# Four attention layers on one core: wol moved into the wo block's slot, wq cut in rows of 2, 2, 1, and the values of the last heads moved forward

## The chip, the core and the metric

The kernel runs on one core of a Trainium2 chip. The metric is device time in microseconds (us) of that core. TensorE is called PE, VectorE DVE, ScalarE ACT; SP is the engine whose queue issues the transfers. PE's granted clock is the share of its full speed that it gets at a moment; in these traces it is 1.0 or 0.5.

## The reference

One token passes four layers: A, B, A, B. Each layer is a norm, a query projection, attention over a cache of 8192 positions in 32 heads of 192, and an output projection.

```python
def attn(x, k_cache, v_cache, wq, wo):           # A and B have the same shapes
    q = (x @ wq).reshape(1, 1, 32, 192).transpose(0, 2, 1, 3)
    p = softmax(einsum("bhqd,bhkd->bhqk", q, k_cache) * 192 ** -0.5)
    o = einsum("bhqk,bhkd->bhqd", p, v_cache)
    return o.transpose(0, 2, 1, 3).reshape(1, 1, 32 * 192) @ wo

x = A_x                                           # 1 x 1 x 640, bfloat16
x = x + attn(layernorm(x), A_k, A_v, A_wq, A_wo)  # "layer 0"
x = x + attn(layernorm(x), B_k, B_v, B_wq, B_wo)  # "layer 1"
x = x + attn(layernorm(x), A_k, A_v, A_wq, A_wo)  # "layer 2"
x = x + attn(layernorm(x), B_k, B_v, B_wq, B_wo)  # "layer 3"
```

One K or V of a head is 3.15 MB. Six such tiles of layers 0 and 1 are kept on the chip for layers 2 and 3; all else is read again.

## The kernel before

SBUF holds a pool of eight slots of one K or V each. A plan lists all transfers in order, and SP issues each as soon as the earlier holders of its slot are done with it. The steps list what the engines do. Here are the parts that the change touches (cuts are marked).

```python
KEPT = {0: {("k", 0), ("v", 0)}, 1: {("v", 28), ("v", 29), ("v", 30), ("v", 31)}}
...
    Q_PARTS = [[(0, 2), (2, 2), (4, 1)] if l < 2 else [(0, 1), (1, 2), (3, 2)] for l in range(NL)]
    NB = 3
...
            elif l == 2:
                plan += [("wq", l, g) for g in range(3)]     # three parts of wq, then K of head 1
                steps.append(("wq", l, 0))
...
                if l == 2 and p == 0:
                    part = [("m", l, 0), ("wq", l, 1), ("s", l, 0), ("v", l, 0), ("wq", l, 2)]
                elif p < H - AHEAD:
                    part = [("m", l, p), ("s", l, p), ("v", l, p)]   # products with K, softmax, values
                else:
                    part = [("m", l, p)]
                    if p > H - AHEAD:
                        part.append(("s", l, p - 1))
                    if p == H - 1:
                        part.append(("s", l, p))
                        part += [("v", l, i) for i in range(H - AHEAD, H)]
                        part.insert(-O_LAST, ("wc", l, 2))
...
        for n in plan:
            if n[0] == "wol" and n[1] + 1 < NL:              # wol shares a slot with the next layer's wq
                m = ("wq", n[1] + 1, 0)
                allot(m)
                before[n] = before[("wq", n[1] + 1, 2)] if n[1] == 0 else before[m]
...
            def q_spread(h):
                c0 = h * DH
```

"wo" is a block of ten heads' rows of the output weights, "wol" the two last heads' rows, "wob" the part of layer 3's last block that is loaded by itself. In layers 2 and 3 wq comes in three parts; a row of it is one of the five rows that each partition holds, 1.47 MB. In layer 2 the slot for K of head 1 is the one that kept K of head 0 holds, so its transfer waits for the products ("m") of head 0 in layer 2.

Of the kernel before, what the change touches and what calls it, by code (L numbers as in the profile page):

```python
# [63 lines left out]
HEADS_W = 10  # L64
# [3 lines left out]
AHEAD = 4  # L68
# [3 lines left out]
def build(nc, A_x, A_k, A_v, A_wq, A_wo, B_x, B_k, B_v, B_wq, B_wo, out):  # L72
# [13 lines left out]
    QW = H * DH  # L86
    Q_PARTS = [[(0, 2), (2, 2), (4, 1)] if l < 2 else [(0, 1), (1, 2), (3, 2)] for l in range(NL)]
    O_PART = [P] * NL
    OI = [O_LAST * DH // n for n in O_PART]
    NB = 3  # L90
    G = 4
# [6 lines left out]
    with ExitStack() as ctx:  # L98
# [14 lines left out]
        oT = sb("oT", [P, NW], BF16)  # L113
        oTl = sb("oTl", [P, max(OI)], BF16)
        o_sb = sb("o_sb", [P, 2 * DH], F32)
# [81 lines left out]
        for l in range(NL):  # L197
            if l < 2:
                plan.append(("wq", l, 0))
                steps += [("wq", l, g) for g in range(3)]  # L200
            elif l == 2:
                plan += [("wq", l, g) for g in range(3)]
                steps.append(("wq", l, 0))
            else:
                plan.append(("wq", l, 0))
                steps.append(("wq", l, 0))
            for p in range(H):
                if p in (HEADS_W, 2 * HEADS_W):
                    b = p // HEADS_W - 1
                    steps += [("wc", l, b), ("wo", l, b)]  # L210
                    plan.append(("wo", l, b))
                if first_load("k", l, p) == ("k", l, p):
                    plan.append(("k", l, p))
                if stays("k", l, p):
                    plan.append(("t", l, p))
# [3 lines that stand above are left out]
                    part = [("m", l, p), ("s", l, p), ("v", l, p)]  # L219
                else:  # L220
                    part = [("m", l, p)]
                    if p > H - AHEAD:
                        part.append(("s", l, p - 1))
                    if p == H - 1:
                        part.append(("s", l, p))
                        part += [("v", l, i) for i in range(H - AHEAD, H)]
                        part.insert(-O_LAST, ("wc", l, 2))
                steps += part
                plan += [n for n in part if n[0] == "v" and first_load(*n) == n]
                if l == 3 and p == 1:  # L230
                    for g in (1, 2):
                        plan.append(("wq", l, g))
                        steps.append(("wq", l, g))
            plan.append(("wo", l, 2))
            steps.append(("wo", l, 2))
            plan.append(("wol", l))
            steps.append(("wol", l))
        plan.append(("wob", NL - 1))
        at = {n: i for i, n in enumerate(steps)}

        def released(n):

            if n[0] in "kvt":
                l, p = n[1:]
                if n[0] != "t" and stays(*n):
                    l, p = n[1] + 2, ORDER[n[1] + 2]["heads"].index(head(*n[1:]))
                return at[("v" if n[0] == "v" else "m", l, p)]
            return at[n]
# [15 lines left out]
        for n in plan:  # L264
            if n[0] == "wol" and n[1] + 1 < NL:
                m = ("wq", n[1] + 1, 0)
                allot(m)
                before[n] = before[("wq", n[1] + 1, 2)] if n[1] == 0 else before[m]
            elif n[0] == "wob":
                before[n] = []  # L270
            elif n not in place:
                allot(n)
# [4 lines left out]
        def wq_rows(l, g):  # L277

            c0, k = Q_PARTS[l][g]
            if l < 2:  # L280
                i = place[("wq", l, 0)] * TS
                return pool[:, i + c0 * QW:i + (c0 + k) * QW].rearrange("p (c n) -> p c n", c=k)
            return slot[place[("wq", l, g)]][:, 0:k * QC].rearrange("p (c n) -> p c n", c=k)

        def wol_rows(l):

            if l + 1 == NL:
                i = place[("wol", l)] * TS
            else:
                i = place[("wq", l + 1, 0)] * TS + (DC * QW if l == 0 else QC)  # L290
            return pool[0:O_PART[l], i:i + OI[l] * D]

        def transfer(n):
# [4 lines left out]
            if n[0] == "wol":  # L298
                r0 = o["wol"] * DH
                if O_PART[l] == P:  # L300
                    return SP.op(lambda s: s.dma_start(
                        wol_rows(l), w["wo"][r0:r0 + O_LAST * DH].rearrange("(p i) n -> p (i n)", p=P)),
                        *free, sem=semOL, inc=16)
                k = O_PART[l] // O_LAST
                for h in range(O_LAST):
                    e = SP.op(lambda s, h=h: s.dma_start(
                        wol_rows(l)[h * k:(h + 1) * k],
                        w["wo"][r0 + h * DH:r0 + (h + 1) * DH].rearrange("(q e i) n -> e q (i n)", e=8, i=OI[l])),
                        *free, sem=semOL, inc=16)
                return e  # L310
            if n[0] == "t":
# [13 lines left out]
            elif n[0] == "wq":  # L325
                c0, k = Q_PARTS[l][n[2]]
                f = lambda s: s.dma_start(
# [52 lines left out]
        def layer(l, ev_z, ev_true):  # L380
# [36 lines left out]
            def q_columns(g):  # L417

                n = ("wq", l, g)
                c0, k = Q_PARTS[l][g]  # L420
                t3 = wq_rows(l, g)[:, :, ORDER[l]["q1"] if l < 2 else 0:]
# [16 lines left out]
            def q_spread(h):  # L438

                c0 = h * DH  # L440
                PE.wait(last["qT"], last["QB"], ev_const)
# [15 lines left out]
            def project(n, rows, o, ev_o):  # L457

                t3 = rows.rearrange("p (i n) -> p i n", n=D)
                k = t3.shape[1]  # L460
                end = n == ("wob", l) or n == ("wol", l) and l + 1 < NL
                PE.wait(ev_o, need(n), last["YB"])
                for i in range(k):
                    for c in range(DC):
                        e = PE.op(lambda t, i=i, c=c, f=y_first[0], fin=end and i == k - 1: t.matmul(  # L465
                            YB[:, c:c + 1], lhsT=t3[:, i, c:D:DC], rhs=o[:, i:i + 1], start=f, stop=fin,
                            skip_group_check=True), signal=(i == k - 1 and c == DC - 1), bank=use["YB"])
                        y_first[0] = False
                freed[n] = e
                return e  # L470
# [65 lines left out]
            def values(h):  # L536
# [16 lines left out]
                if h < H - O_LAST:  # L553
                    parts = [(o_sb[:], OB[par][:, 0:2 * DH])]
                else:
                    q = 1 if O_PART[l] == P else O_PART[l] // O_LAST // 8
                    parts = [(o_sb[:, i * DH:(i + 1) * DH].rearrange("p (i e q) -> p q e i", i=OI[l], q=q),
                              OB[par][:, i * DH:(i + 1) * DH].rearrange("p (q e i) -> p q e i", i=OI[l], q=q))
                             for i in range(2)]
                for o, i in parts:  # L560
                    ev_os[h] = AC.op(lambda a, o=o, i=i: a.activation(o, i, ACT.Copy, scale=rl[pi][:, 0:1]),  # L561
                                     e, ev_rl[h], last["osb"], bank=use[f"O{par}"])
                last["O"][par] = last["rl"][pi] = ev_os[h]

            def gather(h):
# [6 lines left out]
                last["osb"] = e  # L572
                o0 = (h % HEADS_W) * DH
                last["TO"] = last["row_written"] = AC.op(
                    lambda a: a.activation(orow[0:1, o0:o0 + DH], TB[0:1, C_O:C_O + DH], ACT.Copy), e, last["orow"], bank=use["TB"])  # L575

            def gather_last(h):

                n = O_PART[l] // O_LAST
                k = OI[l]  # L580
                r0 = (h - (H - O_LAST)) * n
# [14 lines left out]
            for i, n in enumerate(here):  # L596
# [15 lines left out]
                elif n[0] == "wc":  # L612
                    todo()
                    todo = None
                    columns(NW)
                    last["oTw"] = last["TT"]
                elif n[0] == "wo":
# [3 lines left out]
                    k = NW - NB if n == ("wo", NL - 1, 2) else NW  # L621
                    last["oT"] = project(n, slot[place[n]][:, 0:k * D], oT[:, 0:k], last["oTw"])
                else:
                    last["TT"] = last["TTn"]
                    last["oTl"] = ev_y = project(n, wol_rows(l), oTl[0:O_PART[l]], last["TTn"])
                    if l + 1 == NL:
                        ev_y = project(("wob", l), slot[place[("wo", l, 2)]][:, (NW - NB) * D:NW * D], oT[:, NW - NB:NW], last["oTw"])
                following = [m[2] for m in here[i + 1:] if m[0] == "m" and m[2] not in ev_q][:1]
# [68 lines left out]
```

## Time and profile before

| | |
|---|---|
| time | 1997.24 us, median of 3 (1996.39 to 1998.24) |
| moved by the transfer queue q1 | 848.38 MB, busy 99.4% of the span |
| PE, DVE, ACT busy | 70%, 53%, 11% |

These lines are from the page of the kernel before: the span; the rate in 40 equal slices of 49.9 us; and the queue with packets, MB and its share of sixteen engines' time.

```profile
span 1994.7 us, 20412 instructions
...
GB/s 410 431 431 428 432 429 429 430 431 430 428 430 431 428 432 428 431 429 429 431 382 431 428 431 428 431 430 429 431 429 427 430 430 429 430 429 429 429 432 345
...
q1 hardware_dynamic: 40256, 848.38, 99.4%
```

The kernel is bound by its transfers. Nearly every slice moves 427 to 432 GB/s. Three do not: the first, the 21st and the last. The 21st holds the border of layers 1 and 2. These are its 5 us windows; the columns are the window, its length, then busy time and instructions of PE, PE's weight loads, DVE, ACT and POOL, then PE's granted clock, the transfers' share and GB/s.

```profile
1015.00:1020.00 5.00, 3.44 (x78) 2.96 (x70) 0.00 (x0) 1.11 (x3) 0.00 (x0) 1.00 0.54 227
1020.00:1025.00 5.00, 3.95 (x53) 2.95 (x52) 1.23 (x10) 0.00 (x0) 0.54 (x1) 0.55 0.63 224
1025.00:1030.00 5.00, 3.87 (x53) 1.23 (x44) 4.48 (x3) 0.73 (x2) 0.00 (x0) 0.50 1.00 418
1030.00:1035.00 5.00, 5.00 (x51) 0.89 (x33) 2.88 (x3) 0.00 (x0) 0.00 (x0) 0.92 1.00 422
1035.00:1040.00 5.00, 4.14 (x95) 2.88 (x96) 0.78 (x4) 0.44 (x2) 0.00 (x0) 0.76 1.05 438
```

For about 9 us the rate is halved. The two lines below are the transfer queue's timeline there (start, length, what is issued).

```profile
997.38 29.25 SPq L327 DMA_DIRECT2D pool<-in_A_wq_dram  x3
1034.40 0.34 SPq L322 DMA_DIRECT2D pool<-in_A_k_cache_dram  x1
```

The first line merges three issues: one row of wq at 997.38, and after a long wait two rows at 1021.05 and two at 1026.24. The wait is for the projection of the last wo block, whose slot the second part takes. PE's timeline shows what that projection and the steps after it do; the bracket names the idle time before a line and what ended it.

```profile
1017.86 3.16 PE L465 MATMUL YB<-oT,pool 128*128 128x1 bf16 x75 [0.51 <-DMA pool<-in_B_wo_dram]
...
1024.83 1.39 PE L427 MATMUL QT<-xb,pool 128*128 128x1 bf16 x45
...
1027.34 0.61 PE L508 MATMUL S<-pool,ident 128*128 128x512 bf16 x1 [1.13 <-DVE pool L495]
1027.74 6.63 PE L58 MATMUL S<-pool,ident 128*128 128x512 bf16 x23
```

The projection (first line) waited for the landing of wo, not for PE. The column sums of wq, which make q with 45 matmuls for each row (second line), and the products of head 0 (the last two) follow. When the products end at 1034.37, K of head 1 is issued.

One thing the views above do not print is in the trace's record of semaphore updates. Each transfer reports sixteen times, once for each engine. For the row of wq ahead of the wait the reports come at:

```
1014.2 1014.4 1014.4 1014.5 1014.6 1015.4 1016.7 1019.3 1020.5 1020.5 1020.6 1020.6 1020.7 1020.9 1022.0 1022.4
```

So the fastest engines run dry at 1014.2 and the slowest at 1022.4.

### The profile page before, as it was taken

What the parts mean: (1) busy time and instruction counts of PE and PEld (TensorE: products, weight loads), DVE (VectorE), ACT (ScalarE), POOL (GpSimd) and SP (SyncE); (2) the same over time, 40 slices, a digit from 0 to 9 for tenths busy, and PEclk for the clock granted to TensorE, in tenths of its full rate; (3) what the DMA queues carried; (4) which work ended last, traced back from release to release, by engine and by line L of the source; (5) the groups of instructions that cost most, each with busy time, mean ns of one, the idle gap of its engine ahead of it and who ended that gap; (6) DMA issues with size and microseconds to landing.
All of it is one profiled execution on the core that took longest, in us unless ns stands there. A gap on an engine that the chain in (4) does not pass through costs nothing.

```text
span 1994.7 us, 20412 instructions
## 1 busy us (share of the span) xinstructions
PE 1392.6 (70%) x10438; PEld 318.0 (16%) x7494; DVE 1047.4 (53%) x1074; ACT 220.3 (11%) x665; POOL 4.5 (0%) x22
## 2 busy tenths in 40 slices
PE   4777777667567766767777676777776768767766
PEld 1111111111311111211031111111112212111112
DVE  3554554556255455455726545545663465554563
ACT  0111111110111111111011111111101111111111
POOL 0000000000000000000000000000000000000000
PEclk9888888887688888788878878887897888987889
DMA  9999999999999999999999999999999999999998
GB/s 410 431 431 428 432 429 429 430 431 430 428 430 431 428 432 428 431 429 429 431 382 431 428 431 428 431 430 429 431 429 427 430 430 429 430 429 429 429 432 345
DMA packets 40487, 849.67 MB, mean 426 GB/s; under 512 B 4688, under 2 KB 4688, under 8 KB 5328
## 3 DMA queue, kind: packets, MB, share of 16 engines
q1 hardware_dynamic: 40256, 848.38, 99.4%
q8 instruction: 70, 1.15, 0.2%
q14 instruction: 17, 0.14, 0.0%
q10 hardware_dynamic: 144, 0.00, 0.0%
HBM read 848.36 MB, written 0.00 MB: 425 GB/s over the span
## 4 chain that ended last, share of the span: by engine, by line
DMA 65%; PE 21%; DVE 12%; ACT 1%; issue 1%; another core or an unknown queue 0%; DVEq 0%
DMA pool<-in_B_k_cache_dram 32%; DMA pool<-in_A_k_cache_dram 30%; PE S L58 13%; DVE pool L495 10%; PE O L546 3%; DMA pool<-in_B_wo_dram 2%; PE TB L569 1%; DMA x_bf<-in_A_x_dram 1%; PE S L508 1%; PE YB L465 1%; DVE s_sb L516 1%; ACT p_sb L526 1%; PE QT L427 1%; PE TB L530 1%; DVE small L523 0%
## 5 line engine op out<-in xcount | busy, mean ns | idle before, releaser
L495 DVE TENSOR_TENSOR pool<-pool,q_sb 128x3072 bf16<-128x3072 bf16 x512 | 865.5, 1752 | 406.4 <-DMA pool<-in_A_k_cache_dram 208.3
L58 PE MATMUL S<-pool,ident 128*128 128x512 bf16 x2944 | 797.2, 425 | 35.1 <-DVE pool L495 34.9
L546 PE MATMUL O<-pool,p_sb 128*2 128x384 bf16 x4096 | 346.5, 420 | 1.4 <-DMA pool<-in_B_v_cache_dram 1.4
L508 PE MATMUL S<-pool,ident 128*128 128x512 bf16 x128 | 60.4, 472 | 225.7 <-DVE pool L495 225.5
L516 DVE TENSOR_REDUCE s_sb<-S 128x64 f32<-128x512 f32 x128 | 88.3, 690 | 229.1 <-PE S L58 229.1
L546 PEld LDWEIGHTS O<-pool,p_sb 128*2 128x2 bf16 x4096 | 128.0, 88 | 134.8 <-issue 98.4
L569 PE MATMUL TB<-o_sb,small 128*1 128x192 f32 x480 | 122.8, 389 | 38.2 <-DVE small L534 27.1
L453 ACT ACTIVATE q_sb<-QM 128x192 bf16<-128x192 f32 x120 | 39.6, 330 | 961.2 <-PE QM L446 961.2
L446 PEld LDWEIGHTS QM<-ident,qT 128*128 128x128 bf16 x240 | 23.1, 98 | 741.0 <-issue 725.6
L530 PE MATMUL TB<-small,ones 128*128 128x1 f32 x256 | 49.7, 263 | 109.9 <-ACT p_sb L526 109.9
L520 PE MATMUL QM<-ident,m_bf 128*128 128x128 bf16 x128 | 27.8, 217 | 122.9 <-DVE m_bf L519 121.2
L561 ACT ACTIVATE o_sb<-O,small 128x384 f32<-128x384 f32 (+1 forms) x136 | 77.2, 579 | 233.2 <-PE O L546 233.2
L534 DVE RECIPROCAL small<-TB 128x1 f32<-128x1 f32 x128 | 21.5, 168 | 122.4 <-PE TB L530 122.4
L526 ACT ACTIVATE p_sb<-s_sb,small 128x64 bf16<-128x64 f32 x128 | 44.5, 348 | 266.5 <-DVE small L523 266.5
L523 DVE TENSOR_REDUCE small<-QM 128x1 f32<-128x128 f32 x128 | 37.3, 291 | 62.3 <-PE QM L520 62.3
L575 ACT ACTIVATE orow<-TB 1x192 bf16<-1x192 f32 x120 | 38.3, 319 | 200.7 <-PE TB L569 200.7
L530 PEld LDWEIGHTS TB<-small,ones 128*128 128x128 f32 x256 | 38.9, 191 | 130.4 <-ACT p_sb L526 130.4
L508 PEld LDWEIGHTS S<-pool,ident 128*128 128x128 bf16 x128 | 12.7, 99 | 285.8 <-DVE pool L495 285.8
L520 PEld LDWEIGHTS QM<-ident,m_bf 128*128 128x128 bf16 x128 | 12.3, 96 | 215.3 <-ACT q_sb L453 126.9
L569 PEld LDWEIGHTS TB<-o_sb,small 128*1 128x1 f32 x480 | 33.5, 89 | 81.1 <-DVE small L534 36.0
L465 PE MATMUL YB<-oT,pool 128*128 128x1 bf16 x900 | 38.0, 178 | 5.1 <-DMA pool<-in_A_wo_dram 2.3
L465 PEld LDWEIGHTS YB<-oT,pool 128*128 128x128 bf16 x900 | 37.0, 131 | 5.9 <-ACT oT L479 2.9
(50 smaller groups left out, 215.4 us busy)
## 6 DMA issues: line engine op xcount, KB each, us to landing
pool<-in_B_k_cache_dram SPq DMA_DIRECT2D x64, 3072.0 KB, 35.5
pool<-in_A_k_cache_dram SPq DMA_DIRECT2D x63, 3072.0 KB, 27.6
pool<-in_A_v_cache_dram SPq DMA_DIRECT2D x63, 3072.0 KB, 33.3
pool<-in_B_v_cache_dram SPq DMA_DIRECT2D x60, 3072.0 KB, 37.2
pool<-in_A_wo_dram SPq DMA_DIRECT2D x6, 2400.0 KB, 24.0
pool<-in_B_wo_dram SPq DMA_DIRECT2D x5, 2400.0 KB, 33.3
pool<-in_A_wq_dram SPq DMA_DIRECT2D x1, 7680.0 KB, 20.8
pool<-in_B_wq_dram SPq DMA_DIRECT2D x1, 7680.0 KB, 29.3
```

The source lines that it names most:

```text
L58: return t.add_instruction(mybir.InstMatmult(name=t.bass.get_next_instruction_name(), engine=mybir.EngineType.PE, ins=[t.lower_ap(rhs), t. ...
L453: lambda a: a.activation(q_sb[i][:], QM[:, 0:DH], ACT.Copy), e, last["q"][i], bank=use["QM"])
L465: e = PE.op(lambda t, i=i, c=c, f=y_first[0], fin=end and i == k - 1: t.matmul(YB[:, c:c + 1], lhsT=t3[:, i, c:D:DC], rhs=o[:, i:i + 1], s ...
L495: e = DV.op(lambda v, d0=d0: v.tensor_tensor(k3[:, :, d0:d0 + QD], kin[:, :, d0:d0 + QD], q_sb[qi][:, d0:d0 + QD].unsqueeze(1).broadcast_t ...
L508: t.matmul(S[:, :], lhsT=ident[:], rhs=k3[:, :, d0:d0 + R], start=True, stop=fin) if d0 == 0 else
L516: ev_s = DV.op(lambda v: v.tensor_reduce(s_sb[par][:], S[:].rearrange("p (j r) -> p j r", r=R), AX.X, ALU.add), ev_S[h], last["s"][par], b ...
L520: e = PE.op(lambda t: t.matmul(QM[:, C_MX:C_MX + P], lhsT=m_bf[par][:, 0:1].broadcast_to([P, P]), rhs=ident[:], start=True, stop=True), ev ...
L526: ev_p[h] = AC.op(lambda a: a.activation(p_sb[pi][:], s_sb[par][:], ACT.Exp, bias=negm[par][:, 0:1], accum_out=l_col[par][:]), ev_n, ev_s, ...
L530: e = PE.op(lambda t: t.matmul(TB[:, C_L + par:C_L + par + 1], lhsT=ones[:, 0:1].broadcast_to([P, P]), rhs=l_col[par][:], start=True, stop ...
L546: e = PE.op(lambda e, g=g, j=j, f=m < G, fin=fin: e.matmul(OB[par][32 * g:32 * g + 2, 0:2 * DH], lhsT=p_sb[pi][:, j:j + 2], rhs=t[:, j * D ...
L561: ev_os[h] = AC.op(lambda a, o=o, i=i: a.activation(o, i, ACT.Copy, scale=rl[pi][:, 0:1]), e, ev_rl[h], last["osb"], bank=use[f"O{par}"])
L569: e = PE.op(lambda t, i=i: t.matmul(TB[0:1, C_O:C_O + DH], lhsT=pick[:, i:i + 1], rhs=o_sb[:, i * DH:(i + 1) * DH], start=(i == 0), stop=( ...
```

## The change

It mends which head's q columns layer 3 reads and where a head's output goes in its block (the kernel before passes the comparison with the reference all the same), and means to shorten the border of two layers: wol goes behind wo in wo's slot, which frees room for a second row of wq ahead of the wait; the values of head 28 are computed, and its V loaded, before K of head 31; and the values of head 29 are computed before the last scores. The diff, cut to its core:

```diff
-    Q_PARTS = [[(0, 2), (2, 2), (4, 1)] if l < 2 else [(0, 1), (1, 2), (3, 2)] for l in range(NL)]
-    NB = 3
+    Q_PARTS = [(0, 2), (2, 2), (4, 1)]
+    NB = 7
...
                     if p > H - AHEAD:
                         part.append(("s", l, p - 1))
+                    if p > H - AHEAD + 1:
+                        part.append(("v", l, p - 2))
                     if p == H - 1:
-                        part.append(("s", l, p))
-                        part += [("v", l, i) for i in range(H - AHEAD, H)]
-                        part.insert(-O_LAST, ("wc", l, 2))
+                        part += [("s", l, p), ("wc", l, 2), ("v", l, p - 1), ("v", l, p), ("wo", l, 2)]
...
+            if l + 1 == NL:
+                plan.append(("wob", l))          # and steps: wob now comes before wol
...
+            if n[0] == "wo" and n[2] == 2:
+                return at[("wol", n[1])]         # released(): wo's slot is free after wol
...
         def wol_rows(l):
-            ...
+            return slot[place[("wo", l, 2)]][:, NW * D:(NW + OI) * D]
...
-                c0 = h * DH
+                c0 = head(l, h) * DH - ORDER[l]["q1"] + Q_FIRST * DH
...                                              # values(), heads 30 and 31: one activation for two
-                    parts = [( ... o_sb[:, i * DH:(i + 1) * DH] ... ) for i in range(2)]
+                    o, i = (o_sb[:].rearrange("p (h i e) -> p h e i", h=2, i=OI),
+                            OB[par][:, 0:2 * DH].rearrange("p (h e i) -> p h e i", h=2, i=OI))
```

More of the change, by code (lines that the diff above doesn't have):

```diff
@@ L86, in build @@
     QW = H * DH
-    Q_PARTS = [[(0, 2), (2, 2), (4, 1)] if l < 2 else [(0, 1), (1, 2), (3, 2)] for l in range(NL)]
-    O_PART = [P] * NL
-    OI = [O_LAST * DH // n for n in O_PART]
-    NB = 3
+    Q_PARTS = [(0, 2), (2, 2), (4, 1)]
+    OI = O_LAST * DH // P
+    NB = 7
     G = 4
@@ L113, in build @@
         oT = sb("oT", [P, NW], BF16)
-        oTl = sb("oTl", [P, max(OI)], BF16)
+        oTl = sb("oTl", [P, OI], BF16)
         o_sb = sb("o_sb", [P, 2 * DH], F32)
@@ L223, in build @@
                         part.append(("s", l, p - 1))
+                    if p > H - AHEAD + 1:
+                        part.append(("v", l, p - 2))
                     if p == H - 1:
-                        part.append(("s", l, p))
-                        part += [("v", l, i) for i in range(H - AHEAD, H)]
-                        part.insert(-O_LAST, ("wc", l, 2))
+                        part += [("s", l, p), ("wc", l, 2), ("v", l, p - 1), ("v", l, p), ("wo", l, 2)]
                 steps += part
-                plan += [n for n in part if n[0] == "v" and first_load(*n) == n]
+                plan += [n for n in part if n[0] == "wo" or n[0] == "v" and first_load(*n) == n]
                 if l == 3 and p == 1:
@@ L233, in build @@
                         steps.append(("wq", l, g))
-            plan.append(("wo", l, 2))
-            steps.append(("wo", l, 2))
+            if l + 1 == NL:
+                plan.append(("wob", l))
+                steps.append(("wob", l))
             plan.append(("wol", l))
             steps.append(("wol", l))
-        plan.append(("wob", NL - 1))
         at = {n: i for i, n in enumerate(steps)}
         def released(n):
+            if n[0] == "wo" and n[2] == 2:
+                return at[("wol", n[1])]
             if n[0] in "kvt":
@@ L264, in build @@
         for n in plan:
-            if n[0] == "wol" and n[1] + 1 < NL:
-                m = ("wq", n[1] + 1, 0)
-                allot(m)
-                before[n] = before[("wq", n[1] + 1, 2)] if n[1] == 0 else before[m]
-            elif n[0] == "wob":
+            if n[0] in ("wob", "wol"):
                 before[n] = []
@@ L277, in wq_rows @@
         def wq_rows(l, g):
-            c0, k = Q_PARTS[l][g]
+            c0, k = Q_PARTS[g]
             if l < 2:
@@ L285, in wol_rows @@
         def wol_rows(l):
-            if l + 1 == NL:
-                i = place[("wol", l)] * TS
-            else:
-                i = place[("wq", l + 1, 0)] * TS + (DC * QW if l == 0 else QC)
-            return pool[0:O_PART[l], i:i + OI[l] * D]
+            return slot[place[("wo", l, 2)]][:, NW * D:(NW + OI) * D]
         def transfer(n):
@@ L299, in transfer @@
                 r0 = o["wol"] * DH
-                if O_PART[l] == P:
-                    return SP.op(lambda s: s.dma_start(
-                        wol_rows(l), w["wo"][r0:r0 + O_LAST * DH].rearrange("(p i) n -> p (i n)", p=P)),
-                        *free, sem=semOL, inc=16)
-                k = O_PART[l] // O_LAST
-                for h in range(O_LAST):
-                    e = SP.op(lambda s, h=h: s.dma_start(
-                        wol_rows(l)[h * k:(h + 1) * k],
-                        w["wo"][r0 + h * DH:r0 + (h + 1) * DH].rearrange("(q e i) n -> e q (i n)", e=8, i=OI[l])),
-                        *free, sem=semOL, inc=16)
-                return e
+                return SP.op(lambda s: s.dma_start(
+                    wol_rows(l), w["wo"][r0:r0 + O_LAST * DH].rearrange("(p i) n -> p (i n)", p=P)),
+                    *free, sem=semOL, inc=16)
             if n[0] == "t":
@@ L325, in transfer @@
             elif n[0] == "wq":
-                c0, k = Q_PARTS[l][n[2]]
+                c0, k = Q_PARTS[n[2]]
                 f = lambda s: s.dma_start(
@@ L419, in q_columns @@
                 n = ("wq", l, g)
-                c0, k = Q_PARTS[l][g]
+                c0, k = Q_PARTS[g]
                 t3 = wq_rows(l, g)[:, :, ORDER[l]["q1"] if l < 2 else 0:]
@@ L460, in project @@
                 k = t3.shape[1]
-                end = n == ("wob", l) or n == ("wol", l) and l + 1 < NL
                 PE.wait(ev_o, need(n), last["YB"])
@@ L464, in project @@
                     for c in range(DC):
-                        e = PE.op(lambda t, i=i, c=c, f=y_first[0], fin=end and i == k - 1: t.matmul(
+                        e = PE.op(lambda t, i=i, c=c, f=y_first[0], fin=n[0] == "wol" and i == k - 1: t.matmul(
                             YB[:, c:c + 1], lhsT=t3[:, i, c:D:DC], rhs=o[:, i:i + 1], start=f, stop=fin,
@@ L468, in project @@
                         y_first[0] = False
-                freed[n] = e
+                if n != ("wo", l, 2):
+                    freed[("wo", l, 2) if n[0] == "wol" else n] = e
                 return e
@@ L553, in values @@
                 if h < H - O_LAST:
-                    parts = [(o_sb[:], OB[par][:, 0:2 * DH])]
+                    o, i = o_sb[:], OB[par][:, 0:2 * DH]
                 else:
-                    q = 1 if O_PART[l] == P else O_PART[l] // O_LAST // 8
-                    parts = [(o_sb[:, i * DH:(i + 1) * DH].rearrange("p (i e q) -> p q e i", i=OI[l], q=q),
-                              OB[par][:, i * DH:(i + 1) * DH].rearrange("p (q e i) -> p q e i", i=OI[l], q=q))
-                             for i in range(2)]
-                for o, i in parts:
-                    ev_os[h] = AC.op(lambda a, o=o, i=i: a.activation(o, i, ACT.Copy, scale=rl[pi][:, 0:1]),
-                                     e, ev_rl[h], last["osb"], bank=use[f"O{par}"])
-                last["O"][par] = last["rl"][pi] = ev_os[h]
+                    o, i = (o_sb[:].rearrange("p (h i e) -> p h e i", h=2, i=OI),
+                            OB[par][:, 0:2 * DH].rearrange("p (h e i) -> p h e i", h=2, i=OI))
+                ev_os[h] = last["O"][par] = last["rl"][pi] = AC.op(
+                    lambda a: a.activation(o, i, ACT.Copy, scale=rl[pi][:, 0:1]), e, ev_rl[h], last["osb"], bank=use[f"O{par}"])
             def gather(h):
@@ L572, in gather @@
                 last["osb"] = e
-                o0 = (h % HEADS_W) * DH
+                o0 = (head(l, h) - ORDER[l]["wo"][h // HEADS_W]) * DH
                 last["TO"] = last["row_written"] = AC.op(
@@ L577, in gather_last @@
             def gather_last(h):
-                n = O_PART[l] // O_LAST
-                k = OI[l]
+                n = P // O_LAST
+                k = OI
                 r0 = (h - (H - O_LAST)) * n
@@ L612, in layer @@
                 elif n[0] == "wc":
-                    todo()
-                    todo = None
+                    if todo is not None:
+                        todo()
+                        todo = None
                     columns(NW)
@@ L622, in layer @@
                     last["oT"] = project(n, slot[place[n]][:, 0:k * D], oT[:, 0:k], last["oTw"])
-                else:
+                elif n[0] == "wob":
+                    project(n, slot[place[("wo", l, 2)]][:, (NW - NB) * D:NW * D], oT[:, NW - NB:NW], last["oTw"])
+                else:
+                    if todo is not None:
+                        todo()
+                        todo = None
                     last["TT"] = last["TTn"]
-                    last["oTl"] = ev_y = project(n, wol_rows(l), oTl[0:O_PART[l]], last["TTn"])
-                    if l + 1 == NL:
-                        ev_y = project(("wob", l), slot[place[("wo", l, 2)]][:, (NW - NB) * D:NW * D], oT[:, NW - NB:NW], last["oTw"])
+                    last["oTl"] = ev_y = project(n, wol_rows(l), oTl, last["TTn"])
                 following = [m[2] for m in here[i + 1:] if m[0] == "m" and m[2] not in ev_q][:1]
```

## The prediction

> **What bounds it now.** The transfers. The page's DMA row is at nine tenths in 39 of 40 slices. The q1 queue is busy 99.4% of 16 engines' span moving 848.38 MB at 428 to 432 GB/s in nearly every slice. The Trainium skill, "DMA: Bandwidth & Descriptors", Specifications, gives 435 GB/s as the fabric's ceiling, so the rate has nothing left. The change moves the same bytes, so it can only win idle time of the DMA engines. Little: slices 1, 21 and 40 (410, 382, 345 GB/s). Against 431 GB/s that is about 2.4, 5.7 and 10 us: the start, the border of layers 1 and 2, and the tail after the last data.
>
> **The border 1-2.** Six of eight slots hold kept tiles, so after wo, wol and one row of wq (1.47 MB, issued at 997.4 us in the queue's timeline) nothing can be issued until the wo project ends at 1021.05. The 5 us windows show 227 and 224 GB/s at 1015 to 1025. The timeline shows that project waiting until 1017.86 for wo's landing, not for PE's backlog.
>
> **What the change does there.** (a) wq gets two rows before the stall instead of one: 1.47 MB more, 3.4 us of cover. (b) wq's second part now waits for wol too: +0.7 us (15 matmuls, 0.74). (c) Values of heads 28 and 29 run earlier, but wo's landing ends the wait anyway, so this buys nothing here. (d) After the stall only three rows of wq (10.3 us) remain to bridge until K of head 1, which waits for the products of head 0 (kept K's copy slot; issue at 1034.4). Before, four rows (13.7 us) bridged it, with about 2 us to spare. So I expect most of (a) to be given back: the first hole shrinks to about 2 us, a second opens near 1034 to 1037. PE also does 90 instead of 45 q-column matmuls first, which may delay that issue by about 1 us.
>
> A second reason: the skill's section on why a DMA increments its semaphore by 16 says its engines finish independently and only the full 16 means landed. This trace agrees: for wq's row before the stall the first engine reports at 1014.2, the last at 1022.4. The slowest engine hardly idled; the hole is that of the fast ones. Estimated net gain at the border: 0 to 1.3 us.
>
> **Borders 0-1 and 2-3** show no hole (400 GB/s or more in every window) and keep their slack.
>
> **Tail.** V of head 31 lands at 1983.2; then values 2.7, o_sb 0.94, gather 0.9, 90 projection matmuls 3.8, output 3 us: PE's chain, in both. One ACTIVATE (about 0.58) replaces two (0.94): -0.36 us. wol last instead of wob does not matter: last landing near 1990.1 in both. The head mapping keeps the matmul count.
>
> **Prediction: 1996.2 us, 1992.5 to 1999.0 in 8 of 10.** Faster by over 2%: 0.005; within 2%: 0.99; slower: 0.005.
>
> **Right if:** DMA near 99%, bytes equal; the window rates rise at 1015 to 1025 and fall at 1030 to 1040; K of head 1 in layer 2 is issued between 1034 and 1036; last landing to end unchanged within 0.5 us.
>
> **Wrong if:** the second hole does not open (gain of 2 to 3 us), the engines' lag carried over the border adds up differently in the second half, or an earlier reuse of slots starves the queue at 0-1 or 2-3 (some us slower).

## The result

| | median | runs |
|---|---|---|
| before | 1997.22 us | 1996.39 to 1998.24, 4 runs |
| after | 1998.88 us | 1996.98 to 1999.98, 4 runs |

The ratio is 1.0007, with a 95% interval of 0.999 to 1.0024: the same. Ratios are the mean time of one kernel's fast runs over the mean of the other's in the same rounds, so not quite the ratio of the medians.

The page after, the same lines:

```profile
span 1997.8 us, 20404 instructions
...
GB/s 412 429 430 431 429 429 430 430 430 430 428 431 430 429 431 429 429 431 428 431 369 432 428 429 431 430 429 430 430 430 427 430 428 430 431 426 431 431 429 333
...
q1 hardware_dynamic: 40256, 848.38, 99.3%
```

The bytes are the same to the last digit shown. The slice with the border is slower than before (369 against 382 GB/s), and so is the last (333 against 345). The windows at the border:

```profile
1015.00:1020.00 5.00, 3.75 (x70) 3.67 (x71) 0.00 (x0) 0.79 (x2) 0.00 (x0) 0.50 0.78 326
1020.00:1025.00 5.00, 3.82 (x44) 2.45 (x42) 1.23 (x10) 0.10 (x1) 0.54 (x1) 0.50 0.77 291
1025.00:1030.00 5.00, 3.85 (x94) 2.51 (x91) 4.64 (x3) 0.63 (x2) 0.00 (x0) 0.50 1.01 426
1030.00:1035.00 5.00, 5.00 (x16) 0.00 (x0) 2.12 (x2) 0.00 (x0) 0.00 (x0) 0.60 0.87 296
1035.00:1040.00 5.00, 4.14 (x101) 2.69 (x93) 1.21 (x3) 0.44 (x2) 0.00 (x0) 1.00 0.62 205
```

The first hole is smaller: 326 and 291 instead of 227 and 224 GB/s. A second one has opened at 1030 to 1040, where the kernel before moved 422 and 438. The transfer queue and PE there:

```profile
998.29 30.79 SPq L312 DMA_DIRECT2D pool<-in_A_wq_dram  x3
1036.60 0.34 SPq L307 DMA_DIRECT2D pool<-in_A_k_cache_dram  x1
```

```profile
1017.69 3.16 PE L449 MATMUL YB<-oT,pool 128*128 128x1 bf16 x75 [0.57 <-DMA pool<-in_B_wo_dram]
...
1026.15 2.56 PE L412 MATMUL QT<-xb,pool 128*128 128x1 bf16 x90 [1.28 <-DMA pool<-in_A_wq_dram]
...
1028.57 0.59 PE L493 MATMUL S<-pool,ident 128*128 128x512 bf16 x1
1028.95 7.62 PE L58 MATMUL S<-pool,ident 128*128 128x512 bf16 x23
```

The merged issues are two rows of wq at 998.29, two at 1021.48 and one at 1028.74. K of head 1 is issued 2.2 us later than before. PE does 90 matmuls of column sums instead of 45, and starts them at 1026.15, when the second row has landed; the products start at 1028.57 instead of 1027.34. They also run longer, 7.62 against 6.63 us for the 23 matmuls, since the granted clock rose from 0.5 to 1.0 at 1034.0 us here and at 1030.8 before.

The tail of the two kernels is compared next: the values of the last head on PE, the activation in which ACT scales them, the gather in which PE turns them into columns, and the last addition. Before:

```profile
1983.22 2.73 PE L546 MATMUL O<-pool,p_sb 128*2 128x384 bf16 x32 [1.41 <-DMA pool<-in_B_v_cache_dram]
...
1986.00 0.94 ACT L561 ACTIVATE o_sb<-O,small 128x192 f32<-128x192 f32 x2 [3.99 <-PE O L546]
...
1987.00 0.86 PE L585 MATMUL TB<-small,o_sb 128*64 128x1 f32 x12 [1.05 <-ACT o_sb L561]
...
1991.59 0.16 DVE L633 TENSOR_TENSOR x_bf<-small,YB 128x5 bf16<-128x5 f32 x1 [20.06 <-PE YB L465]
```

After:

```profile
1985.29 2.73 PE L531 MATMUL O<-pool,p_sb 128*2 128x384 bf16 x32 [3.97 <-DMA pool<-in_B_v_cache_dram]
...
1988.07 0.91 ACT L544 ACTIVATE o_sb<-O,small 128x384 f32<-128x384 f32 x1 [6.55 <-PE O L531]
...
1989.03 1.44 PE L566 MATMUL TB<-small,o_sb 128*64 128x1 f32 x12 [1.02 <-ACT o_sb L544]
...
1994.20 0.16 DVE L618 TENSOR_TENSOR x_bf<-small,YB 128x5 bf16<-128x5 f32 x1 [18.77 <-PE YB L449]
```

The values begin in both at the landing of the last V. The one activation takes 0.91 us, hardly less than the two (0.94). The gather takes 1.44 instead of 0.86 us. From the start of the values to the end of the last addition it is 1991.59 + 0.16 - 1983.22 = 8.53 us before, and 9.07 after. In the trace of after the clock stays at 0.5 from 1982.9 to the end; before, it fell at 1983.1, but was back at 1.0 from 1986.5 to 1989.9. So both began the last values at half clock (2.73 us each). PE idled 3.97 us for the last V, against 1.41 before, since in the new order it has nothing left to do; this one pair does not show that the longer wait kept the clock down. a_order_old tests the order below.

### The profile page after: what moved, and what is told of

Same layout as the page of the kernel before. It is cut to its first block, busy times and chain, and to the rows that moved or that the text cites. A ratio compares the mean times of both kernels' runs of the same rounds, so it can differ in the third digit from the quotient of the medians.

```text
span 1997.8 us, 20404 instructions
## 1 busy us (share of the span) xinstructions
PE 1390.6 (70%) x10438; PEld 319.0 (16%) x7494; DVE 1048.1 (52%) x1074; ACT 220.0 (11%) x657; POOL 4.5 (0%) x22
## 3 DMA queue, kind: packets, MB, share of 16 engines
q1 hardware_dynamic: 40256, 848.38, 99.3%
## 4 chain that ended last, share of the span: by engine, by line
DMA 67%; PE 18%; DVE 12%; ACT 1%; issue 1%; another core or an unknown queue 1%; DVEq 0%
DMA pool<-in_B_k_cache_dram 32%; DMA pool<-in_A_k_cache_dram 32%; PE S L58 12%; DVE pool L480 11%; PE O L531 2%; DMA pool<-in_A_wo_dram 2%; DMA pool<-in_A_wq_dram 1%; DMA x_bf<-in_A_x_dram 1%; PE S L493 1%; PE TB L550 1%; PE QT L412 1%; ACT p_sb L511 1%; DVE s_sb L501 1%; PE YB L449 1%
## 5 line engine op out<-in xcount | busy, mean ns | idle before, releaser
L531 PE MATMUL O<-pool,p_sb 128*2 128x384 bf16 x4096 | 341.1, 416 | 8.0 <-DMA pool<-in_B_v_cache_dram 6.9
L544 ACT ACTIVATE o_sb<-O,small 128x384 f32<-128x384 f32 x128 | 77.1, 602 | 236.1 <-PE O L531 236.1
```

Of the source, the lines that this page charges most:

```text
L531: e = PE.op(lambda e, g=g, j=j, f=m < G, fin=fin: e.matmul(OB[par][32 * g:32 * g + 2, 0:2 * DH], lhsT=p_sb[pi][:, j:j + 2], rhs=t[:, j * D ...
L544: lambda a: a.activation(o, i, ACT.Copy, scale=rl[pi][:, 0:1]), e, ev_rl[h], last["osb"], bank=use[f"O{par}"])
```

## The experiments

Three theories were open.

- A, rows and bridge: two rows shrink the first hole, but only three rows are left to bridge the time until K of head 1 can be issued, so a second hole takes the gain back.
- B, order: the new order of values lets PE idle and cool, and that costs.
- C, slowest engine: only the slowest transfer engine counts, and it has no hole to lose, so nothing at the border matters much.

Twelve experiments ran, nine new kernels and three repeats, each five times, with the kernel before in the same rounds. All gave correct results. They ran in three calls, each on another chip: after_again, a_rows122, a_order_old and a_like3; then a_warm and the three b_ runs; then before_again, a_like3_rows122, a_like3_again and a_warm10. Kernels are compared only within the same rounds. No interval, each about 0.12% or 2.5 us to either side, excludes 1. The kernel before against itself came out 0.28 us apart, so differences of means below about 0.5 us are not read here. The traces tell more than the times. For each profile the table has the idle time of the transfers' fastest engine at the border. It is worked out from the first of the sixteen reports of successive transfers, from the row of wq ahead of the wait to the fourth transfer after it: the distance of two reports less the transfer's own time, which is 7.30 us for a K or V (the distance of successive reports when no hole is near) and in proportion to the bytes for rows of wq (6.84 us for two, 3.42 for one).

| kernel | rows of wq | after the first part come | idle: first hole, later ones | last V landed | mean time less mean of before, same rounds |
|---|---|---|---|---|---|
| before (first profile) | 1, 2, 2 | wq | 8.8, 0.3 | 1983.2 | |
| before_again | 1, 2, 2 | wq | 8.6, 0.4 | 1982.7 | -0.28 |
| after (first profile) | 2, 2, 1 | wq | 6.1, 4.8 | 1985.2 | +1.42 (4 runs) |
| after_again | 2, 2, 1 | wq | 6.4, 3.5 | 1983.8 | +0.69 |
| a_rows122 | 1, 2, 2 | wq | 9.5, 0.2 | 1983.6 | +0.12 |
| a_order_old | 2, 2, 1 | wq | 5.7, 3.8 | 1983.7 | -0.34 |
| a_like3 | 2, 2, 1 | K, V of head 1 | 5.7, 1.7 | 1981.6 | -1.13 |
| a_like3_again | 2, 2, 1 | K, V of head 1 | 6.2, 0.5 | 1980.9 | -1.73 |
| a_like3_rows122 | 1, 2, 2 | K, V of head 1 | 9.3, 0.2 | 1983.7 | +0.78 |
| b_like3_old | 2, 2, 1 | K, V of head 1 | 5.8, 1.1 | 1982.4 | -1.63 |
| b_like3_old_tail | 2, 2, 1 | K, V of head 1 | 5.9, 1.0 | 1981.2 | -1.83 |
| b_like3_warm_tail | 2, 2, 1 | K, V of head 1 | 5.8, 1.3 | 1982.3 | -0.99 |
| a_warm | 2, 2, 1 | wq | 6.3, 3.2 | 1983.1 | +1.32 |
| a_warm10 | 2, 2, 1 | wq | 6.4, 3.7 | 1984.3 | +1.06 |

### after_again: the changed kernel as reference

> The changed kernel once more, as the reference of this call. All theories: about 1998 us, 0 to 2 us over the kernel before, and K of head 1 of layer 2 issued 36 to 37 us after the 1000 us mark in the profile (1036.6 in the first trace), with transfer rates under 300 GB/s in both 1020-1025 and 1030-1040.

It ran at 1998.19 us (before: 1997.58). K of head 1 was issued at 1035.73, a little before what was expected; both holes were there (289 GB/s at 1020 to 1025, 312 and 277 at 1030 to 1040).

### a_rows122: rows of 1, 2, 2 again

```diff
-    Q_PARTS = [(0, 2), (2, 2), (4, 1)]
+    Q_PARTS = [[(0, 2), (2, 2), (4, 1)] if l < 2 else [(0, 1), (1, 2), (3, 2)] for l in range(NL)]
```

(with the index of the layer where it is read)

> The changed kernel with wq of layers 2 and 3 in parts of 1, 2, 2 rows again, all else as changed. Theory A (what two rows win in the first hole is lost in a second one, because only three rows bridge to K of head 1): the first hole is back (two 5 us windows near 225 GB/s), the second is gone (no window of 1030-1045 under 400), K of head 1 is issued near 1034.5 to 1036, its landing is 1 to 2 us earlier than in the changed kernel, and the time is 1 to 2 us under it, about 1997. Rival B (the new order of the values costs, by letting TensorE idle and fall to half clock): the time stays within 0.5 us of the changed kernel.

It ran at 1997.45 us, 0.56 us under after_again in the means. Three of its windows:

```profile
1020.00:1025.00 5.00, 3.95 (x55) 2.94 (x54) 1.24 (x10) 0.08 (x1) 0.54 (x1) 0.50 0.54 183
...
1030.00:1035.00 5.00, 5.00 (x18) 0.10 (x1) 2.14 (x2) 0.00 (x0) 0.00 (x0) 0.73 1.01 429
1035.00:1040.00 5.00, 4.14 (x123) 3.39 (x124) 1.37 (x4) 0.44 (x2) 0.00 (x0) 0.95 1.09 456
```

As theory A has it, the first hole is back in full and the second is gone. K of head 1 was issued at 1035.27 and reported first at 1044.65; in after_again at 1044.91, though that kernel had moved 1.47 MB more ahead of the wait. The gain in time that was expected, 1 to 2 us, was not reached: 0.56 us is near what five rounds can tell, so here the trace decides, and it says that with this loading order two rows and one row bring K of head 1 at about the same moment.

### a_order_old: values of heads 28 and 29 after the last scores again

```diff
-                    if p > H - AHEAD + 1:
-                        part.append(("v", l, p - 2))
                     if p == H - 1:
-                        part += [("s", l, p), ("wc", l, 2), ("v", l, p - 1), ("v", l, p), ("wo", l, 2)]
+                        part += [("s", l, p), ("v", l, p - 3), ("v", l, p - 2), ("wc", l, 2), ("v", l, p - 1), ("v", l, p), ("wo", l, 2)]
```

> The changed kernel with the values of heads 28 and 29 computed, and loaded, after K31 and the last scores again, all else as changed. Rival B: the granted clock is 1.0 again in 1010-1015 and in part of 1985-1990 as in the kernel before, K of head 1 is issued about 1 us earlier than in the changed kernel, landing of the last V to the end takes 8.6 instead of 9.1 us, and the time is 1 to 2 us under the changed kernel. Theory A: both holes stay as in the changed kernel, the time moves by at most 0.7 us.

It ran at 1997.25 us, 1.03 us under after_again in the means. Both holes stayed (305, 310 and 308 GB/s in the windows from 1020, 1030 and 1035), so they are not the order's. The granted clock was 1.0 from 1977.0 to 1990.6. The values of the last head took 1.47 us instead of 2.73; they began 1.13 us after the landing of the last V, PE being still at work, and from that landing to the last addition's end it took 8.37 us against 9.13 in after_again. The values of the last head, the gather and the last addition:

```profile
1984.84 1.47 PE L529 MATMUL O<-pool,p_sb 128*2 128x384 bf16 x32
1987.33 0.86 PE L564 MATMUL TB<-small,o_sb 128*64 128x1 f32 x12 [1.02 <-ACT o_sb L542]
...
1991.92 0.16 DVE L616 TENSOR_TENSOR x_bf<-small,YB 128x5 bf16<-128x5 f32 x1 [18.52 <-PE YB L447]
```

So B holds in the tail, with 0.76 us, and not at the border, where K of head 1 reported at 1044.58. The other profiles agree. In all six with the new order and no added matmuls (after, after_again, a_rows122 and the three a_like3 runs) the clock had fallen before the last V landed, did not come back, and landing to last addition took 9.12 to 9.13 us, though PE's idle time before the last values went from 0.4 to 4.0 us. In the five with the old order (the two before, this one, b_like3_old and b_like3_old_tail) it took 8.25 to 8.57 us. In the means of this call the order is worth at least as much as the changed kernel is slower by (0.69 us); that the two are the same thing is not shown, as a_rows122 wins 0.56 us too.

### a_like3: layer 2 loaded as layer 3 is

```diff
-            elif l == 2:
-                plan += [("wq", l, g) for g in range(3)]
-                steps.append(("wq", l, 0))
...
-                if l == 2 and p == 0:
-                    part = [("m", l, 0), ("wq", l, 1), ("s", l, 0), ("v", l, 0), ("wq", l, 2)]
-                elif p < H - AHEAD:
+                if p < H - AHEAD:
...
-                if l == 3 and p == 1:
+                if l >= 2 and p == 1:
```

The slots of wo and of the first rows of wq then take K and V of head 1, and the rest of wq goes where the kept K and V of head 0 lay.

> The changed kernel with layer 2 loaded as layer 3 is: after the first two rows of wq come K and V of head 1, and the other three rows after them, so nothing before them waits for the products of head 0. Theory A: 6.3 MB instead of 4.4 MB follow the first hole without such a wait, so the second hole closes (no window of 1030-1045 under 400 GB/s) while the first stays as small as in the changed kernel; the time falls by 2 to 4 us against the changed kernel, to 1994 to 1996.5, a little under the kernel before too. Rival B: at most 0.5 us. Rival C (only the slowest transfer engine counts, and it has no hole): at most 1 us under the kernel before, whatever the holes of the others.

It ran at 1996.29 us (before: 1997.58). Windows, and the queue's timeline:

```profile
1020.00:1025.00 5.00, 3.51 (x36) 2.14 (x34) 1.23 (x10) 0.40 (x2) 0.54 (x1) 0.50 0.85 319
...
1030.00:1035.00 5.00, 5.00 (x14) 0.00 (x0) 1.81 (x2) 0.00 (x0) 0.00 (x0) 0.54 0.94 338
1035.00:1040.00 5.00, 3.01 (x29) 0.74 (x23) 1.64 (x5) 0.44 (x2) 0.00 (x0) 1.00 0.94 394
```

```profile
1021.18 0.34 SPq L302 DMA_DIRECT2D pool<-in_A_k_cache_dram  x1
1028.92 0.33 SPq L302 DMA_DIRECT2D pool<-in_A_v_cache_dram  x1
1036.97 4.33 SPq L307 DMA_DIRECT2D pool<-in_A_wq_dram  x2
```

K of head 1 now goes out at 1021.18, V at 1028.92 and wq only at 1036.97. The first hole is as small as in the changed kernel. The second is much smaller but not gone, against what was expected (338 and 394 GB/s): V waits for the column sums of the first two rows, and these for the slowest engine's landing at 1026.3. The idle sum falls from 9.9 to 7.4 us, and the last V lands 2.2 us earlier than in after_again. The mean time is 1.8 us under after_again, a little less than the 2 to 4 expected, and the runs of the two do not overlap (1995.73 to 1997.00 against 1997.52 to 1999.06). That speaks for A. Against C, which allowed at most 1 us under the kernel before, the 1.13 us of this run say little; the later runs with this loading order and two rows (0.99 to 1.83 us under it) say more.

### a_like3_rows122 and a_like3_again: the fourth corner

The first is a_like3 with the rows of a_rows122, the second a_like3 unchanged.

> Layer 2 loaded as layer 3 is, with wq in parts of 1, 2, 2 rows: the fourth corner of rows times loading order. Theory A (two rows are worth something where no second hole can take it back): the first hole is as deep as in the kernel before (two windows of 1015-1025 near 225 GB/s or less), no window of 1025-1045 is under 390, and the time is 1 to 2 us over the same loading order with two rows (below, same call), near that of the kernel before. If the rows are worth nothing in themselves: within 0.4 us of it.

> Layer 2 loaded as layer 3 is, two rows first, once more for this call: 1 to 1.6 us under the kernel before, as in the first call; last V landed 1 to 2 us earlier than in the kernel before's profile of this call.

They ran at 1998.23 and 1995.53 us: 2.51 us apart in the means, and the five runs of one do not overlap with those of the other (1997.78 to 1998.49, 1995.19 to 1996.31). Windows of the first:

```profile
1020.00:1025.00 5.00, 3.95 (x55) 2.92 (x54) 1.24 (x10) 0.05 (x1) 0.54 (x1) 0.50 0.58 186
...
1030.00:1035.00 5.00, 5.00 (x17) 0.00 (x0) 2.17 (x2) 0.00 (x0) 0.00 (x0) 0.70 0.94 403
1035.00:1040.00 5.00, 2.49 (x38) 1.15 (x36) 3.19 (x6) 1.00 (x3) 0.00 (x0) 1.00 0.98 420
```

The same windows of a_like3_again:

```profile
1020.00:1025.00 5.00, 3.95 (x52) 2.78 (x50) 1.24 (x10) 0.00 (x0) 0.54 (x1) 0.50 0.78 297
...
1030.00:1035.00 5.00, 5.00 (x19) 0.00 (x0) 2.46 (x2) 0.00 (x0) 0.00 (x0) 0.78 0.96 372
1035.00:1040.00 5.00, 3.01 (x39) 1.11 (x35) 2.93 (x5) 0.44 (x2) 0.00 (x0) 0.91 0.96 411
```

In a_like3_rows122 there is no second hole, and the first is as deep as before (186 GB/s). The four corners, as means less the kernel before in the same rounds (the two rows of the table come from two calls, so read along a row first):

| | rows 1, 2, 2 | rows 2, 2, 1 | what two rows do |
|---|---|---|---|
| wq before K of head 1 | +0.12 | +0.69 | +0.56 |
| K and V of head 1 before the rest of wq | +0.78 | -1.73 (-1.13 in the first call) | -2.51 |

Two rows ahead of the wait are worth about 2.5 us where the next transfers do not wait for the products of head 0, and nothing where they do. Nor does the loading order gain alone. This settles theory A. The sixteenth report of each transfer, the one that says all has landed, agrees. Worked out with it as the idle time above was with the first, the four transfers lose 3.1 us in a_like3_rows122 and 0.4 in a_like3_again (1.0 in a_like3), and with wq first 3.2 with one row (a_rows122) and 3.1 with two (after_again). So even the slowest reports have time to lose at the border, and the premise of C, that they have none, fails. That only they count is not excluded: 3.1 and 0.4 us differ by about as much as the times. The 2.5 us are less than the 3.4 us that a row takes to transfer; the idle sums of the two (9.5 and 6.7 us) differ by 2.8.

### before_again: the kernel before against itself

> The kernel before against itself, to see what five rounds can tell apart, and for a second profile of it. All theories: ratio within 0.0005 of 1; in the profile the first values of the last head start to the last addition in 8.4 to 8.6 us, K of head 1 of layer 2 issued 34 to 35.5 us after the 1000 us mark.

Ratio 0.9999; 0.28 us between the means. K of head 1 at 1034.12. From the landing of the last V to the last addition 8.56 us (8.57 in the first profile); from the start of the values it was 7.62, not 8.4 to 8.6, as here the values began 0.94 us after the landing and ran at the full clock. So before, too, there are two kinds of tail, equally long.

### a_warm and a_warm10: keeping PE's clock up

The added matmuls are idle work: the values of the last head overwrite what they write.

```diff
+                if l == NL - 1 and h == H - 1:
+                    PE.wait(ev_p[h], last["O"][par])
+                    for _ in range(24):          # 10 in a_warm10
+                        PE.op(lambda t: t.matmul(OB[par][:, 0:2 * DH], lhsT=ident[:], rhs=wq0[1][:, 0, :], start=True, stop=True),
+                              signal=False, bank=use[f"O{par}"])
                 PE.wait(need(nv_), ev_p[h], last["O"][par])
```

> The changed kernel with 24 idle matmuls (128x384, into the bank that the values of the last head are about to overwrite) on TensorE while it waits for the last V; they read a tile that nothing writes any more and change no result. Theory D (in the new order TensorE has caught up before the last V lands, idles, falls to half clock, and its last chain of work is slower for it): the granted clock is 1.0 at the last V's landing and the time from that landing to the end falls from about 12.4 us to 11.5, the whole by 0.7 to 1 us. Rival (the tail is longer for its order of wol and wob, or for the merged activation): landing to end stays within 0.2 us of 12.4.

> The changed kernel with 10 idle matmuls in the wait for the last V instead of 24, which in the first try ran 2.8 us past its landing. Theory D (clock): values of the last head take 1.5 instead of 2.7 us, they start within 0.3 us of the landing, and from that start to the last addition it takes 7.2 to 8.0 us instead of 9.1; the time falls by 0.7 to 1.8 us against the changed kernel of the first call, to 1996.5 to 1997.7. If the clock has fallen all the same: 9.1 us.

Both missed their times: 1998.43 and 1998.24 us, no faster than the changed kernel. The tail of a_warm:

```profile
1981.87 4.07 PE L530 MATMUL O<-wq,ident 128*128 128x384 bf16 x24
...
1985.88 1.47 PE L536 MATMUL O<-pool,p_sb 128*2 128x384 bf16 x32
...
1992.96 0.16 DVE L623 TENSOR_TENSOR x_bf<-small,YB 128x5 bf16<-128x5 f32 x1 [17.90 <-PE YB L449]
```

With the clock at 1.0 until 1990.4 the values take 1.47 us and all to the last addition 7.24 us instead of 9.07. So the clock does set the length of the tail. But the 24 matmuls ran 2.8 us past the last V's landing (1983.11) and cost more than they won. With ten of them the clock fell at 1984.9, 0.6 us after the landing: the values took 2.21 us, and the tail from the landing 8.60 us, against 9.13 in after_again. No gain in time came of it. How many idle matmuls would win something was not found; it depends on when the last V lands, which moved by more than 1 us between profiles.

### b_like3_old, b_like3_old_tail, b_like3_warm_tail: loading order, order of values and early projection together

The first has the edits of a_like3 and a_order_old. The second also projects the first rows of wo before the gather of the last head:

```diff
                 elif n[0] == "wo":
-                    if todo is not None:
+                    if todo is not None and n != ("wo", NL - 1, 2):
...
                 elif n[0] == "wob":
+                    todo()
+                    todo = None
```

The third is a_like3 with that edit and the 24 idle matmuls.

> Layer 2 loaded as layer 3 is, and the values of heads 28 and 29 after the last scores as in the kernel before. If the two effects add (border 1.5 to 2 us, tail 0.9 us): 1995.2 to 1996 us, landing of the last V to the end 11.6 us, last V landed near 1981.6.

> The same, and in the last layer the first eight rows of wo are projected before the gather of the last head instead of after it, in the time of that head's activation. Landing of the last V to the end 10.8 to 11.3 us; the time 0.3 to 0.8 us under the run without it, 1994.6 to 1995.5, and 0.1% under the kernel before.

> Layer 2 loaded as layer 3 is, the changed kernel's order of values, the idle matmuls before the last values, and the early projection. If clock and order are exchangeable in the tail: within 0.5 us of the kernel with the old order and the early projection; landing of the last V to the end 10.8 to 11.3 us.

They ran at 1995.61, 1995.55 and 1996.15 us (before, same rounds: 1996.81; the means differ by 1.63, 1.83 and 0.99). In the tail the early projection shortens the time from the start of the values to the last addition from 7.24 to 6.25 us, but in that profile PE was 2.0 us late at the last V, so from its landing it was 8.26 and 8.25. From landing to the end it was 11.53, 11.62 and 11.41 us in the three, where 10.8 to 11.3 was expected of the last two. Of the 0.3 to 0.8 us expected of the early projection nothing can be told: the means differ by 0.20. The third came out 0.84 us over the second, where at most 0.5 was expected. The five runs with K and V of head 1 first and two rows of wq, four kernels, all came out 1.0 to 1.8 us under the kernel before; b_like3_old_tail, furthest under it, by 0.1%. Each interval still includes 1.

## Why the prediction was right

The time, predicted at 1996.2 us within 1992.5 to 1999.0, was 1998.88. "Within 2%" held. That the time lies in the range says little by itself: the range is 6.5 us wide, the effects argued over are 1 to 3 us, and the forecast had the sign of the net effect wrong (1 us faster than before, measured 1.4 us slower in the means, which is not clear of noise). Of the four conditions under "Right if" two held, the bytes and the window rates. Two failed in the profile: K of head 1 was issued at 1036.60, not between 1034 and 1036, and from the last landing to the end it took 5.68 us instead of 4.61, where a change of 0.5 was allowed. So the mechanism of the second hole was right, and the sizes around it came out right partly by luck.

- **What bounds it.** Right: the same bytes, 99.3% after against 99.4%.
- **The second hole.** Right, and the main point. It was forecast near 1034 to 1037 and showed at 1030 to 1040; two rows' gain was given back. The four corners show it by experiment.
- **The net at the border.** A gain of 0 to 1.3 us was forecast; K of head 1 first reported 1.6 us later than before in the first profile and 0.6 in the second (1045.89 and 1044.91, against 1044.29). By the prediction's own count against 431 GB/s, the 21st slice is 7.2 us short instead of 5.7: the first hole shrinks from 4.8 to 2.8 us, and the second adds 4.2. The term that was too small is the delay of K's issue: "about 1 us", measured 2.2 and 1.3 us (1036.60 and 1035.73, against 1034.40; the forecast window ended at 1036). It left out PE's clock, which rose 3.2 us later than before in the first profile. How late it rises was different in each profile.
- **The tail.** "One ACTIVATE (about 0.58) replaces two (0.94)" failed: the merged one takes 0.91 us. 0.58 is the time of the plain one of the same size; the merged one reorders elements as the two did. And "PE's chain, in both" left out PE's clock, which in the new order had fallen before the last V and stayed down: 9.07 instead of 8.53 us in the first profiles. So -0.36 us was forecast and about +0.5 to +0.8 measured.
- **The slowest engine.** "The slowest engine hardly idled" may be true of the idling (1022.4 to about 1023), but as "a second reason" for little gain it was too strong. The last reports before and after the first hole, 1022.40 and 1031.58, are 9.2 us apart for two rows that take 6.84, so the full landing lost 2.3 us there too. Where no second hole opened, two rows won 2.5 us.
- **Borders 0-1 and 2-3.** Right: no window of the changed kernel there is under 396 GB/s.

Left open: what wol in wo's slot and seven columns of wob are worth by themselves, and whether the order and the rows add up; a_rows122 and a_order_old each undo one and their differences of 0.56 and 1.03 us sum to more than the changed kernel is slower by in that call (0.69).

## What to carry to other kernels

When a stall ahead of a wait is filled with work taken from behind it, ask what the queue lives on until the next dependence is met: here three rows could not bridge what four had. Change the order first, so that what follows the wait depends on nothing late, and then the extra prefetch pays: here 2.5 us of 1998, about 0.1%. And before an engine's backlog is cleared ahead of its last input, see whether the idle time will cost it its clock.

## What the Trainium skill lacked or had wrong

- "DMA: Bandwidth & Descriptors", the section on why a DMA increments its semaphore by 16, says that the engines finish independently. It has no figure for how far they drift apart in a queue that never runs dry. Here the reports of one transfer spread over 2 us at 57 us and over 8.3 us at 1010 us, in steps of about 1.5 us for one engine at a time; a hole sets the spread back to 1.7. The steps keep company with the 70 instruction packets of 16 KB that the kernel before fetches. Between the mean reports of successive K and V transfers, the sixteen delays together grew by 1.47 us on average in the 57 stretches in which such a packet started, and by 0.08 in the 180 in which none did; in 55 of the 57 at most one engine shifted. No run moved the packets, so that they cause the steps is not tested by experiment.
- The same page's Specifications give about 358 GB/s as the limit of HBM for one core. One core alone read 425 GB/s over the whole span here. The row is a share of two cores that stream at once; the same page's Bandwidth section and "HBM Reference" have about 425 GB/s for a core that streams alone.
- "TensorE: Matmul & The Clock Gate", Part 1, says the clock has two states and windows of about 3.4 us. The traces agree: 0.5 and 1.0, in stretches of 3.4, 6.8, 10.2, 13.7 us and more. It does not say how far narrow matmuls count as busy. Here 90 weight loads and matmuls of one column filled PE from 1026.15 to 1028.7 and dense matmuls from 1028.57 on, yet the clock rose only at 1034.0; and 90 of them, from 1990.4 to 1994.2, did not raise it.
- No page has the cost of an activation that reorders elements: 128x384 took 0.91 us with reordering and 0.58 without.
